# Reordering the start of an attention-plus-mixer kernel: masks first, a third decay buffer, weight conversions and products placed by hand

## The chip, the cores and the metric

One core of one Trainium2 chip. The metric is the device time of one execution in microseconds (us). Engines are named as the profile names them: PE is TensorE's matmul side, PEld its weight loads, DVE is VectorE, ACT is ScalarE, POOL is GpSimd, SP issues the DMAs. The median time of several runs is called "the median". Positions inside an execution ("103.57") are microseconds from the start of the profiled run, which is one run among several.

## The reference

An RWKV6 recurrence per head, followed by an MLP mixer over tokens and then over channels, all in float32 (the mixer's weights arrive as float64):

```python
batch, n_heads, seq, head_dim = (4, 8, 768, 48)
state = np.zeros((B, H, D, D))
for t in range(S):
    cur = np.einsum('bhd,bhe->bhde', u[None] * kt, vt)
    y[:, :, t] = np.einsum('bhd,bhde->bhe', rt, state + cur)
    state = wt[:, :, :, None] * state + np.einsum('bhd,bhe->bhde', kt, vt)
# ... y becomes x: (B, S, H*D) = (4, 768, 384)
h = np.maximum(xt @ w_tok1, 0.0) @ w_tok2          # over tokens, d_tok 256
u = x + h.transpose(0, 2, 1)
h2 = np.maximum(u @ w_ch1, 0.0) @ w_ch2            # over channels, d_ch 1536
return u + h2
```

## The kernel before

The attention is cut into 12 units, three to a batch element, of 256 tokens each. `levels(i)` makes the weights within a unit: a first block (`begin` scales r and k on ScalarE, `gram0` multiplies them, a masked copy on VectorE picks the result), then five further levels, each with a gram on PE, a *join* on VectorE (r and k multiplied by decays) and another masked copy (plain copies on ScalarE at the last two levels). `post(i)` then does the transposes, the products kv, the states, the part of y that comes from the states (`before`), a tiny copy `seen` on ScalarE (two words per partition), and the part of y from within the unit (`within`).

The first batch element (units 0 to 2) also has to convert the float64 weights. One "pair" is two pieces of 512 columns, each with one exponent step on ScalarE (L170) and five steps on VectorE (L169, 171, 172, 173, 175). There are three pairs for the token weights (`to_tok`; the texts call them pairs 1, 2 and 3, in Python `to_tok[0]` to `[2]`) and nine for the channel weights (`to_ch`).

```python
# the order of emission below, with the scheduler's own choices,
# sets the order of each engine's queue
for n, t in enumerate((rs[i % 3], ks[i % 3], ws[i % 3])):   # load_rkw
    sp.dma_start(t[rows], rkw[i, n, rows, :])
# ...
masks.append(m8)                                  # six casts on VectorE
for i, t in enumerate(weights_at):
    (dve if i == 0 else pool).memset(t, 0.0)
# ... levels(i), begin():
decay = apool.tile([128, COLS // 2], f32, name="decay")          # two buffers
rp = L["rp"] = apool.tile([128, COLS], f32, name="rp")
kp = L["kp"] = apool.tile([128, COLS], f32, name="kp", bufs=1)   # one buffer
# ... post(i), at the end of before():
seen = apool.tile([128, 2], f32, name="seen")
act.copy(seen, y[:, :, UC * A * D - 1])           # within() waits for it
# ... mixing():
def hidden(i, c):   # one w_tok1 product, 12 per batch element: 2 sums of 6
    ...
def back(c):        # two w_tok2 products, then x += on VectorE (the add, L430)
    ...
# ... the first batch element:
emit(woven(levels(0), levels(1)))
load_v(0); load_rkw(2); load_v(1); load_v(2)
p0, p1, p2 = post(0), post(1), post(2)
p1[3:3] = hiddens[0] + hiddens[1]
p2[3:3] = hiddens[2] + hiddens[3]
emit(woven(levels(2), p0 + p1, to_tok[:2]))
emit(woven(p2, to_tok[2:]))
emit(hiddens[4] + hiddens[5])
# then: six back products and turns woven with to_ch[:2], then the up products
# (z_ps), the down products, and units 3 to 11 woven into the mixing of the rest
```

Of the kernel before, what the change touches and what calls it, by code (L numbers as in the profile page):

```python
# [10 lines left out]
f32 = mybir.dt.float32  # L11
# [18 lines left out]
COLS = UC * A * 128  # L30
# [7 lines left out]
def woven(*lists):  # L38

    keyed = []  # L40
    for n, pieces in enumerate(lists):
        total, at = sum(c for c, _ in pieces), 0.0
        for i, (c, f) in enumerate(pieces):
            keyed.append(((at + c / 2) / total, n, i, c, f))
            at += c
    return [(c, f) for *_, c, f in sorted(keyed, key=lambda e: e[:3])]


def emit(pieces):
    for _, f in pieces:  # L50
        f()
# [3 lines left out]
def rwkv6_then_mixer(  # L55
# [22 lines left out]
    nc = tc.nc  # L78
    pe, dve, act, pool, sp = nc.tensor, nc.vector, nc.scalar, nc.gpsimd, nc.sync

    const = ctx.enter_context(tc.tile_pool(name="const", bufs=1))
    wts = ctx.enter_context(tc.tile_pool(name="wts", bufs=1))
    vpool = ctx.enter_context(tc.tile_pool(name="vpool", bufs=3))
    apool = ctx.enter_context(tc.tile_pool(name="apool", bufs=2))
# [8 lines left out]
    rs = [const.tile([128, COLS], f32, name=f"r{i}") for i in range(3)]  # L93
    ks = [const.tile([128, COLS], f32, name=f"k{i}") for i in range(3)]
    ws = [const.tile([128, COLS], f32, name=f"w{i}") for i in range(3)]
    weights_at = [const.tile([128, 2, UC * A, T], f32, name=f"at{i}") for i in range(3)]
    vs = {}

    def load_rkw(i):
        if i >= NU:  # L100
            return
        for n, t in enumerate((rs[i % 3], ks[i % 3], ws[i % 3])):
            for rows in (slice(0, 128),) if i < 3 else (slice(0, D), slice(P, P + D)):
                sp.dma_start(t[rows], rkw[i, n, rows, :])

    def load_v(i, queue=sp):
        if i >= NU:
            return
        vs[i] = vpool.tile([128, UC, DM], f32, name="vt")
        b, j = divmod(i, UB)  # L110
        queue.dma_start(vs[i], v[b, ts(j, UC * 128), :].rearrange("(c p) e -> p c e", p=128))

    u_col = const.tile([128, A], f32, name="u_col")
    act.dma_start(u_col, u)
    load_rkw(0)
    load_rkw(1)



    masks = []  # L120
    for l in range(4):
# [7 lines left out]
        n, x = (T, 1) if l == 0 else (32, UC * A)  # L129
# [2 lines left out]
        for j in range(2):  # L132
            dve.tensor_copy(m8[ts(j, T)], flat[ts(j, T), ts(j, n)].unsqueeze(1).to_broadcast([T, x, n]))
        masks.append(m8)
    for i, t in enumerate(weights_at):
        (dve if i == 0 else pool).memset(t, 0.0)
    ident = const.tile([128, 128], f32, name="ident")
    make_identity(nc, ident)

# [48 lines left out]
    def conversion(*weights):  # L188
        pieces = [e for w in weights for e in blocks(*w)]
        return [(0.2, lambda n=n: convert(pieces[n:n + 2], n)) for n in range(0, len(pieces), 2)]  # L190
# [6 lines left out]
    def levels(i):  # L197
# [5 lines left out]
        products = []  # L203

        def begin():
            decay = apool.tile([128, COLS // 2], f32, name="decay")
            L["w"] = apool.tile([128, UC, A, 2], f32, name="w_chunk", bufs=4)
            pool.memset(L["w"], 0.0)
            products.extend([w_, decay, w_[:, :COLS // 4], decay[:, :COLS // 8], w_[:, :COLS // 16],
                             decay[:, :COLS // 32], L["w"].rearrange("p c a j -> p (c a j)")])  # L210

            rp = L["rp"] = apool.tile([128, COLS], f32, name="rp")
            kp = L["kp"] = apool.tile([128, COLS], f32, name="kp", bufs=1)
            both = [(t.rearrange("p (n two) -> p n two", two=2)[:ROWS], x.rearrange("p (n two) -> p n two", two=2)[:ROWS], o)
                    for t, x, o in ((rp, r_, 1), (kp, k_, 0))]
            for t, x, o in both:
                act.copy(t[:, :, o], x[:, :, o])
            for t, x, o in both:
                t, x = (e[:, :, 1 - o].rearrange("p (c a n) -> p c a n", c=UC, a=A) for e in (t, x))
                for a in range(A):  # L220
                    act.mul(t[:, :, a, :], x[:, :, a, :], u_col[:ROWS, a:a + 1])  # L221
# [76 lines left out]
        def block(l):  # L298
            gram(l)
            join(l, products[l], products[l + 1])  # L300
            pick(l)

        pieces = [(0.1, begin), (1.6, first_block)]
        for l in range(1, LEVELS):
            pieces.append((1.2, lambda l=l: block(l)))
        return pieces

    def post(i):
# [69 lines left out]
        def within():  # L378
# [9 lines left out]
            for n in range(2):  # L388
                act.copy(x[ts(n, P), 1], got[ts(1 - n, P), 1])  # L389

        return [(1.0, tokens), (1.1, carry), (0.1, update), (1.1, before), (1.1, within),
                (0.01, lambda: load_rkw(i + 3)), (0.01, lambda: load_v(i + 3))]


# [9 lines left out]
    def weight_sums():  # L404
        t1, t2, t4 = w_sums
        dve.tensor_sub(t1, w12, w11)
        dve.tensor_sub(t2, w22, t1)
        dve.tensor_sub(t4, w21, t2)
# [121 lines left out]
    def beside(after, ahead):  # L530

        tokens, carry, update, before, within, *loads = after
        begin, first, *rest = ahead

        def one(*pieces):
            return (sum(c for c, _ in pieces), lambda: emit(pieces))

        return [begin, tokens, one(carry, first), update, one(before, rest[0]), one(within, rest[1]), *loads, *rest[2:]]


    hiddens, turned, ups, downs = mixing(0)
    hiddens = [list(e) for e in zip(*hiddens)]
    to_tok = conversion((wtok1, w_tok1, 2, 256), (wtok2, w_tok2, 2, 256))
    to_ch = conversion((wch1, w_ch1, 1, 512), (wch2, w_ch2, 4, 128))
    emit(woven(levels(0), levels(1)))
    load_v(0)
    load_rkw(2)
    load_v(1)
    load_v(2)
    p0, p1, p2 = post(0), post(1), post(2)  # L550
    p1[3:3] = hiddens[0] + hiddens[1]
    p2[3:3] = hiddens[2] + hiddens[3]
    emit(woven(levels(2), p0 + p1, to_tok[:2]))
    emit(woven(p2, to_tok[2:]))
    emit(hiddens[4] + hiddens[5])


    for bt in range(B):
        if bt == 0:
            emit(woven(turned, to_ch[:2]))  # L560
            both = [f for e in zip(ups[0], ups[1]) for f in e]
            emit(woven(both, to_ch[2:7]))
            emit(woven(downs[0][:-4], to_ch[7:]))
            weight_sums()
            pieces = downs[0][-4:] + [(0.01, weight_difference)] + downs[1] + ups[2] + downs[2]
        else:
            hiddens, pieces, ups, downs = mixing(bt)
            pieces = [(3.9, lambda h=h: emit(h)) for h in hiddens] + pieces
            for s in range(S // SEG):
                pieces += ups[s] + downs[s]  # L570
        n = (bt + 1) * UB
        if n < NU:
            att = levels(n) if bt == 0 else []
            for i in range(n, n + UB):
                att += beside(post(i), levels(i + 1)) if i + 1 < NU else post(i)
            emit(woven(att, pieces))
        else:
            emit(pieces)
# [29 lines left out]
```

## Time and profile before

| | before |
|---|---|
| median (4 runs) | 627.34 us (626.74 to 627.84) |
| profiled run | 625.85 us, span 624.1 us |
| first level-1 gram on PE | 15.68 |
| states of unit 2, 12 steps (L350) | 78.05 to 80.24 |
| first add to end of sixth (L430) | 91.47 to 102.87 |
| first up product (z_ps, L443) | 103.57 |
| from there to the end | 520.5 us |

The page, the stages and the chain of this run are in the prediction below. This is the timeline of the kernel before, cut to one stretch. Each line has start, length, engine, source line, operation, output and inputs, count, and in brackets the idle time of the engine just ahead and what ended it:

```profile
78.05 2.19 DVE L350 SCALAR_TENSOR_TENSOR state<-state,w_chunk,kv_ps 128x48 f32<-128x48 f32 x12 [1.51 <-PE kv_ps L333]
...
81.68 0.16 ACT L376 COPY seen<-y_ps 128x2 f32<-128x2 f32 x1 [1.22 <-PE y_ps L370]
81.90 1.96 PE L383 MATMUL y_ps<-vt,at 64*64 64x48 f32 x64
83.64 1.68 PE L256 MATMUL gram<-r,k 48*64 48x32 f32 x52
85.42 4.17 PE L421 MATMUL h_ps<-x,wtok 128*128 128x384 f32 x8
91.47 0.56 DVE L430 TENSOR_TENSOR x<-x,h_ps 128x384 f32<-128x384 f32 x1 [0.92 <-PE h_ps L428]
103.57 4.70 PE L443 MATMUL z_ps<-xT,wch 128*128 128x256 f32 x21
```

Read it from top to bottom as one path: states of unit 2, `seen`, 64 products within the unit, then a gram (of unit 3, which fills PE while ScalarE copies y into x), the last eight matmuls of w_tok1, the adds, and the first up product. The change works on every link of it.

### The profile page before, as it was taken

How to read it: one execution, taken by the hardware profiler on the slowest of the kernel's cores; microseconds unless marked ns; L12 is line 12 of the kernel's file. 1: busy time of each engine (PE TensorE's matmuls, PEld its weight loads, DVE VectorE, ACT ScalarE, POOL GpSimd, SP SyncE). 2: the span in 40 equal slices, each digit the busy share in tenths (PEclk: the TensorE clock that was granted, in tenths of full speed). 3: DMA queues.
4: the chain of work that ended last, by engine and by line, in shares of the span. 5: the costliest groups of instructions: out<-in, count | busy, mean ns of one | idle time of the engine just before them, and what ended most of it. 6: DMA issues, size and time to landing. Idle time of an engine off the chain costs nothing.

```text
span 624.1 us, 19852 instructions
## 1 busy us (share of the span) xinstructions
PE 591.5 (95%) x8980; PEld 500.7 (80%) x8980; DVE 341.5 (55%) x743; ACT 201.6 (32%) x500; POOL 7.2 (1%) x32
## 2 busy tenths in 40 slices
PE   2888788999999999999999999999999999999997
PEld 2867556876888896789889896789899885898987
DVE  5889799996766783436364362526243331040403
ACT  6064554520355433432323312332212411202020
POOL 4000000000000000000000000000000000000000
PEclk9996679999999999999999999999999999999999
DMA  8236564610232222111111100000000000000000
GB/s 344 105 80 213 162 197 141 221 43 27 65 94 79 54 67 66 30 50 27 53 45 60 27 28 27 1 2 3 26 2 27 2 27 1 0 1 26 16 12 26
DMA packets 19380, 38.63 MB, mean 62 GB/s; under 512 B 2112, under 2 KB 12864, under 8 KB 19296
## 3 DMA queue, kind: packets, MB, share of 16 engines
q1 hardware_dynamic: 19152, 37.36, 19.0%
q8 instruction: 70, 1.15, 0.8%
q14 instruction: 14, 0.11, 0.1%
q10 hardware_dynamic: 144, 0.00, 0.0%
HBM read 32.64 MB, written 4.72 MB: 60 GB/s over the span
## 4 chain that ended last, share of the span: by engine, by line
PE 88%; DVE 6%; ACT 3%; issue 1%; DMA 1%; SPq 0%; DVEq 0%; ACTq 0%
PE z_ps L443 30%; PE q_ps L477 25%; PE gram L256 8%; PE h_ps L428 5%; PE h_ps L421 5%; PE h_ps L453 3%; PE y_ps L383 2%; PE y_ps L370 2%; PE kv_ps L333 2%; PE gram L233 2%; PE kT_ps L323 1%; PE xT_ps L435 1%; PE gram L250 1%; DVE state L350 1%; DMA w<-in_rkw_dram 1%
## 5 line engine op out<-in xcount | busy, mean ns | idle before, releaser
L443 PE MATMUL z_ps<-xT,wch 128*128 128x256 f32 x864 | 195.3, 382 | 0.0
L443 PEld LDWEIGHTS z_ps<-xT,wch 128*128 128x128 f32 x864 | 161.4, 190 | 22.4 <-ACT z L445 0.7
L445 ACT ACTIVATE z<-z_ps 128x256 f32<-128x256 f32 x144 | 55.0, 382 | 159.4 <-PE z_ps L443 145.7
L477 PE MATMUL q_ps<-wch,z 128*128 128x192 f32 x528 | 93.6, 329 | 0.0
L477 PEld LDWEIGHTS q_ps<-wch,z 128*128 128x128 f32 x528 | 86.3, 190 | 1.3
L477 PE MATMUL q_ps<-scratch,z 128*128 128x192 f32 x396 | 71.1, 330 | 0.0
L256 PEld LDWEIGHTS gram<-r,k 48*64 48x64 f32 x3072 | 59.4, 153 | 13.0 <-issue 7.2
L256 PE MATMUL gram<-r,k 48*64 48x32 f32 x3072 | 64.6, 235 | 4.1 <-issue 1.8
L477 PEld LDWEIGHTS q_ps<-scratch,z 128*128 128x128 f32 x396 | 64.3, 190 | 0.9 <-ACT kT L324 0.2
L288 DVE TENSOR_TENSOR k<-k,decay 112x512 f32<-112x512 f32 x36 | 24.9, 691 | 46.1 <-PE gram L256 34.6
L469 DVE TENSOR_TENSOR z<-z 128x768 f32<-128x768 f32 x11 | 10.5, 958 | 63.5 <-ACT z L445 63.4
L288 DVE TENSOR_TENSOR k<-k,w 112x512 f32<-112x512 f32 x36 | 24.8, 690 | 35.6 <-PE gram L256 30.0
L428 PE MATMUL h_ps<-h,wtok 128*128 128x384 f32 x96 | 37.0, 510 | 3.8 <-DVE x L430 2.0
L350 DVE SCALAR_TENSOR_TENSOR state<-state,w_chunk,kv_ps 128x48 f32<-128x48 f32 x160 | 30.7, 258 | 17.3 <-PE kv_ps L333 17.3
L421 PE MATMUL h_ps<-x,wtok 128*128 128x384 f32 x96 | 37.5, 541 | 1.7 <-ACT x L389 1.6
L430 DVE TENSOR_TENSOR x<-x,h_ps 128x384 f32<-128x384 f32 x24 | 13.3, 555 | 36.6 <-PE h_ps L428 36.3
L233 PE MATMUL gram<-rp,kp 48*64 48x64 f32 x768 | 22.5, 248 | 10.9 <-ACT kp L221 8.2
L272 DVE COPY_PREDICATED at<-mask,gram 128x512 f32<-128x512 uint8 x36 | 32.3, 898 | 0.0
L233 PEld LDWEIGHTS gram<-rp,kp 48*64 48x64 f32 x768 | 18.4, 154 | 15.4 <-ACT kp L221 10.7
L421 PEld LDWEIGHTS h_ps<-x,wtok 128*128 128x128 f32 x96 | 19.2, 208 | 13.5 <-ACT x L389 2.0
L280 ACT COPY at<-gram 16x256 f32<-16x256 f32 x48 | 17.4, 363 | 36.3 <-PE gram L256 35.1
L428 PEld LDWEIGHTS h_ps<-h,wtok 128*128 128x128 f32 x96 | 16.4, 189 | 15.5 <-DVE x L430 3.3
(80 smaller groups left out, 563.0 us busy)
## 6 DMA issues: line engine op xcount, KB each, us to landing
scratch<-in_w_ch_dram SPq DMA_DIRECT2D x10, 512.0 KB, 4.4
vt<-in_v_dram SPq DMA_DIRECT2D x12, 384.0 KB, 3.7
out_dram<-o SPq DMA_DIRECT2D x24, 192.0 KB, 1.9
x<-in_w_ch_dram SPq DMA_DIRECT2D x8, 512.0 KB, 4.4
w<-in_rkw_dram SPq DMA_DIRECT2D x18, 192.0 KB, 3.3
k<-in_rkw_dram SPq DMA_DIRECT2D x18, 192.0 KB, 3.1
r<-in_rkw_dram SPq DMA_DIRECT2D x18, 192.0 KB, 3.5
scratch<-in_w_tok_dram SPq DMA_DIRECT2D x4, 512.0 KB, 9.2
```

Of the source, the lines that this page charges most:

```text
L233: pe.matmul(g[cols, q, ts(a, T)], L["kp"][rows, tokens], L["rp"][rows, tokens], start=True, stop=True)
L256: fours(lambda q, j, rows, cols: pe.matmul(g[cols, q, ts(ca, 32)], k_[rows, ds(ca * 128 + j * T, T)], right[rows, ts(2 * ca + j, 32 // b), ...
L272: dve.copy_predicated(out=dst, data=g.rearrange("p q (m b) -> p q m b", b=b), mask=masks[l].rearrange("p x t -> p (x t)").rearrange("p (m ...
L280: act.copy(at[p:p + b, :, :, n * 2 * b + b:(n + 1) * 2 * b], g[p:p + b, :, :, ts(n, b)])
L288: dve.tensor_mul(left, left, wv[:, :, 1].unsqueeze(2).to_broadcast([ROWS, n, b]))
L350: dve.scalar_tensor_tensor(new[:, a], state[bt, g][:, a], L["w"][:, c, a, j:j + 1], got[:, a], op0=ALU.mult, op1=ALU.add)
L421: pe.matmul(sums[i], wtok1[:, c, ts(i, 128)], xs[bt][:, c, :], start=(c == 0), stop=(c == C - 1))
L428: pe.matmul(ps, wtok2[:, i, ts(c, 128)], h1[:, i, :], start=(i == 0), stop=(i == DTOK // 128 - 1))
L443: pe.matmul(ps, wch1[:, m, ts(jt, 128)], xT[:, m, ts(s, SEG)], start=(m == 0), stop=(m == DM // 128 - 1))
L445: act.activation(zs[s][:, jt, :], ps, AF.Relu)
L453: pe.matmul(ps, zs[0][:, jt, ts(n, 128)], wch2[:, jt, :], start=(jt == 0), stop=(jt == NJ - 1))
L477: pe.matmul(ps, a[:, j, :], b[:, j, :], start=(j == 0), stop=(j == HJ - 1))
```

## The change

The intent: have the mask casts out of the way when the first gram is ready; let decays run ahead; keep conversions out of the way of unit 2's joins; use the room at unit 2's joins and states for token pairs 2 and 3; and put w_tok1 products into unit 2's post. Two helpers pin the order of issue: `newest` notes an engine's latest instruction, `behind` makes later pieces stand behind it in that engine's queue without any semaphore.

```diff
+    def newest(*engines):
+        return {e.engine: next(ins.name for ins in reversed(block.instructions) if ins.engine == e.engine)
+                for e in engines}
+
+    def behind(marks, pieces):
+        ...   # each instruction of the pieces is ordered after marks[its engine]
@@
+    for t in weights_at:
+        dve.memset(t, 0.0)
@@ load_rkw
-        for n, t in enumerate((rs[i % 3], ks[i % 3], ws[i % 3])):
+        for n, t in ((1, ks[i % 3]), (2, ws[i % 3]), (0, rs[i % 3])):
@@ after the masks
-    for i, t in enumerate(weights_at):
-        (dve if i == 0 else pool).memset(t, 0.0)
+    masked = newest(dve)
@@ begin
-            decay = apool.tile([128, COLS // 2], f32, name="decay")
+            decay = apool.tile([128, COLS // 2], f32, name="decay", bufs=3)
@@ the first batch element
-    emit(woven(levels(0), levels(1)))
+    emit(behind(masked, woven(levels(0), levels(1))))
     ...
-    p1[3:3] = hiddens[0] + hiddens[1]
-    p2[3:3] = hiddens[2] + hiddens[3]
-    emit(woven(levels(2), p0 + p1, to_tok[:2]))
-    emit(woven(p2, to_tok[2:]))
+    l2, joined = levels(2), {}
+    l2.append((0.01, lambda: joined.update(newest(dve))))
+    emit(woven(l2, p0 + p1, to_tok[:1]))
+    tokens, carry, update, before, within, *loads = p2
+    emit([tokens, *hiddens[0], carry])
+    emit(behind(joined, to_tok[1:2]))
+    emit([update])
+    updated = newest(dve)
+    emit(hiddens[1] + [before] + hiddens[2] + [within] + hiddens[3] + loads)
+    attended = newest(pe)
+    emit(behind(updated, to_tok[2:]))
     emit(hiddens[4] + hiddens[5])
@@ batch loop
-            att = levels(n) if bt == 0 else []
+            att = behind({**updated, **attended}, levels(n)) if bt == 0 else []
```

In what follows, **the opening** is the first part (memsets, casts first, load order, `behind(masked, …)`), **the decay** is the third buffer, and **the placing** is everything from `l2, joined` on, the last line included.

## The prediction

> **What bounds the kernel now.** I read the page's first two parts for the engines and the stages, then the chain that ended last in order of time, then windows by stage and the timeline of the first 105 us. The page:
>
> ```profile
> PE 591.5 (95%) x8980; PEld 500.7 (80%) x8980; DVE 341.5 (55%) x743; ACT 201.6 (32%) x500; POOL 7.2 (1%) x32
> PE   2888788999999999999999999999999999999997
> DVE  5889799996766783436364362526243331040403
> PEclk9996679999999999999999999999999999999999
> ```
>
> One slice is 15.6 us. TensorE is full from slice 7 on (104 us), and everything the change could win lies in the first seven slices, where VectorE is at 8 to 9 and TensorE has gaps. The windows say it in us (columns: busy time and instructions of PE, PEld, DVE, ACT, POOL, then clock, DMA share, GB/s):
>
> ```profile
> 8.00:44.00 36.00, 28.52 (x932) 26.00 (x936) 31.85 (x65) 16.61 (x44) 0.00 (x0) 1.00 0.48 167
> 44.00:90.00 46.00, 38.09 (x958) 28.93 (x950) 41.87 (x110) 23.02 (x54) 0.34 (x3) 0.70 0.60 183
> 90.00:104.00 14.00, 11.33 (x44) 6.49 (x43) 12.28 (x25) 6.69 (x16) 0.00 (x0) 1.00 0.42 130
> 104.00:150.00 46.00, 46.00 (x233) 35.66 (x233) 41.48 (x72) 16.26 (x37) 0.00 (x0) 1.00 0.34 109
> ```
>
> PE's idle time before 104 us is 8.2 + 7.5 + 7.9 + 2.7 = 26 us; after it, 520 us hold some 6.4 us of idle. VectorE is idle for 10 us between 8 and 104. So the end is set by when the first `up` product (z_ps, L443) starts, now 103.6 us, plus a TensorE-bound rest which the change does not touch in kind. The chain shows the alternation ahead of it (start, length, what):
>
> ```profile
> 10.20 0.70 DVE decay L290
> 11.88 1.33 DVE at L239 x2
> 15.68 2.78 PE gram L256 x94
> 68.53 1.65 PE h_ps L421 x2
> 78.05 2.20 DVE state L350 x12
> 85.39 0.53 ACT scratch L170
> 97.67 0.57 DVE x L430
> 103.73 31.48 PE z_ps L443 x144
> ```
>
> The readings are that the opening waits on VectorE (the mask casts, run from 8.59 to 11.9 beside the decay products, hold the first masked copies back), that unit 2's states come late (78.05), since two conversions of token weights stand in VectorE's queue between unit 2's joins, and that channel-weight conversions (L170, L173) then mix with the back products.
>
> [...] the decay product ran at 10.20 although its input was read by the join at 7.38, because six casts stood ahead. So the order of issue, which this change pins, is worth as much as the dependencies. [...] the clock in the windows 48-50 and 50-54 is 0.50. [...] the clock column reads 1.00 from 0 to 44 us, yet a gram of 64 matmuls takes 1.97 us there (23.49) against 1.14 us at 149 us, so I take the opening for half clock as well. [...]
>
> **Part 1: masks first, three memsets on VectorE, k before w before r.** VectorE has 5.4 us of wait before 7.38; in it now go 3 memsets of 0.91 (two were GpSimd's) and the casts, 1.59 + 0.58. They need the masks, and GpSimd, freed of its memsets, should end at about 5.4. VectorE is then free at about 6.2. That takes 2.2 us off the path from the first join to the first masked copy. But a load of 512 KB takes 1.28 us (first ready at 4.74, 5.99, 7.38), so r of unit 0 comes at 7.25 in place of 4.7, and ScalarE's queue now reads: kp copy and 4 scalings (0.65 + 1.33), rp copy at 7.3, 4 scalings to 9.3, then **kp of unit 1, which has a single buffer** and waits for the last of unit 0's 64 products. Those end at 9.3 + 0.3 + 1.1 = 10.7. Then kp copy 0.65, rp copy 0.65, rp scalings 1.3: unit 1's first product at 13.6, its last at 14.6 + 0.3 + 1.1 = 16.0, against 15.1 now. The gram of level 1 starts there: 16.0 against 15.68. **Sum: +0.3 us**; the casts' gain is eaten by the load order and the single kp.
>
> **Part 2: three decay buffers.** Unit 2's first decay product and first join (0.65 each) move from 33 to 39 us into the opening, at about 16. VectorE then is ahead by 1.3 us at 38 us, less the r join that stays. It removes no wait of the chain: **about 0 to -0.5 us**.
>
> **Part 3: the placing of token pairs and products.** The compiled order, engine by engine, shows VectorE doing pair 1 as now, then unit 2's levels 1 to 5 without a conversion between levels 3 and 5, then pair 2 around the last join, the states of unit 2, pair 3, and only then unit 3's first block. I walk VectorE's new queue with the durations of the old trace (join half 0.61, masked copy 0.65, level 1's 1.28, 12 state steps 2.17, 16 steps 2.88, a conversion step pair 0.7, 0.7, 1.2, 1.2, 1.2). From 38.3: level 1's join at 48.5 (now 49.3). There y of unit 0 and its within products are put before most of the level-2 gram on TensorE, at half clock 1.95 us each, so level 2's join comes at 54.4 (now 53.7), and level 3's, after two products of w_tok1 (0.73 each warm, 1.5 cold), at 59.9 (now 58.3). VectorE idles some 2.5 and 3.4 us there, since pair 2's work no longer fills the gap. Level 5's join then comes at 68 to 69, now 71.04: without pair 2 ahead of it **2.5 us are won**. Of that ScalarE takes back: its queue has the exponent step of pair 2 ahead of the one-word copy `seen` that frees the within products of unit 1, and w_tok1 products of unit 1 stand ahead of unit 2's kv. The states of unit 2 come at 76 to 77.3 (now 78.05), the last w_tok1 product ends at 87.6 to 89 (now 89.6). One exponent step (0.7) no longer stands between the two ReLUs of h1. First L430: 88.7 to 90.5 against 91.47. **Sum: -1 to -2.8 us.**
>
> **Part 4: what was displaced.** In the old order 7 us of channel-weight conversion lie before the first L430. In the new one none does, so it falls among the six L430 (0.5 each): between the second and third stand 4.3 us of conversion steps, between the fourth and the sixth 5.5. TensorE needs 2.45 us from one back product to the next, so it waits. From the first L430 to the end of the sixth: two pairs at 5.0 + 6 x 0.5 + one wait of 0.9 = 13.9 us, now 91.47 to 102.87 = 11.4. **Sum: +2.5 us.** After that VectorE is one pair (5 us) behind, ending its conversions at 138 in place of 132.6. That is hidden: the last channel weights are first read 8 x 1.18 = 9.4 us into the down products, which start at 135.2.
>
> **The sum.** +0.3 - 0.3 - 1.9 + 2.5 = +0.6 us: a first `up` product at 104.2, 627.8 us. It is a long walk with some ten waits, good to 3 us.
>
> **Rivals.** (1) *The clock.* Half clock shows in 47-57, 66-76 and 83-88 us, some 20 us of PE work which would take about 11 at full clock. [...] one spell of 10 us spared gives 3 to 5 us, of which perhaps half on the chain. [...] Against: new waits of VectorE for TensorE mean that neither overlaps better. Time then: 623 to 625. (2) *VectorE stays the bound and all is moved, not removed.* Its work before 132 us is the same, plus 1.8 us of memsets in idle time. For it: DVE at 8 to 9 tenths until slice 9. Then 627 to 628. (3) *Back products stall more than I say*, because scratch and spare are loaded late: the first channel pair's buffers come free only after pair 3 (about 85), and a load of two took some 4.5 us. Then the first up product comes at 106 to 107, and the time is 630. (4) *The opening wins its 2 us after all*, if ScalarE's kp of unit 1 isn't held. Then 625 or 626.
>
> **Range and chances.** The walk gives 627.8. Rival 1 seems to me the likelier of the departures (one in two, -4), rivals 3 and 4 one in five each (+2.5, -2). That makes 627.8 - 2.0 + 0.5 - 0.4 = 625.9. The range is 5 to either side: 620.5 to 631. A gain of over 2% is 12.5 us, half of all the idle time ahead of 104 us, for a change that removes no work: 0.03. A loss of as much would need stalls far beyond rival 3: 0.02.
>
> **What would show it right or wrong.** In the changed kernel: VectorE free of casts by 6.3 us, the first masked copy at 9.6 to 10, but the first level-1 gram between 15.5 and 16.3. The states of unit 2 (12 steps) at 76 to 77.5. First L430 (a few lines lower in the new source) at 88.7 to 90.5. The third L430 over 4 us after the second, with PE waiting for VectorE there. First z_ps product between 101 and 106.5, and from there to the end 520 us as now. It is wrong if the first z_ps product comes before 99 us (the clock or pair 2's place won more), if the opening ends over 1.5 us earlier, or if the rest after it isn't 520 us, which would mean that the later order of decays and joins counts.

## The result and the profile after

| | before | after |
|---|---|---|
| median (4 runs each) | 627.34 us | 630.21 us (629.19 to 630.57) |
| profiled run | 625.85 us | 630.19 us |

The ratio of the times is 1.0044, with a 95% interval of 1.0026 to 1.0061: within 2%, but slower. A ratio here is the mean time of one kernel's fast runs over that of the other's fast runs of the same rounds, so it is not quite the ratio of the medians quoted. The profiled run of the kernel before is faster than all four runs of its median, so the two profiles differ by 4.3 us where the medians differ by 2.9.

Three of the lines of the page that the prediction shows, for the changed kernel:

```profile
PE 591.7 (94%) x8980; PEld 500.6 (80%) x8980; DVE 343.3 (55%) x745; ACT 201.1 (32%) x500; POOL 6.6 (1%) x30
DVE  7886769999676783635454471616344341040403
PEclk9996769999999999999999999999999999999999
```

PE's busy time is the same (591.5 and 591.7), so nothing was added or taken away: the time lost is waiting. VectorE is emptier in the fourth and the sixth slice (47 to 63 and 79 to 94 us: 6 tenths in place of 9) and fuller in the tenth (141 to 157 us: 9 in place of 6). The windows put it in numbers, with the columns of the prediction's windows:

```profile
8.00:44.00 36.00, 28.13 (x912) 25.78 (x916) 31.05 (x58) 16.65 (x44) 0.00 (x0) 1.00 0.47 167
44.00:90.00 46.00, 34.66 (x905) 26.70 (x898) 34.60 (x92) 20.42 (x49) 1.50 (x3) 0.73 0.56 165
90.00:104.00 14.00, 12.77 (x101) 7.21 (x100) 9.71 (x21) 6.68 (x14) 0.00 (x0) 0.93 0.27 92
104.00:150.00 46.00, 44.23 (x188) 34.73 (x188) 46.00 (x85) 18.45 (x40) 0.00 (x0) 1.00 0.43 138
```

Between 44 and 90 us VectorE did 34.60 us of work in place of 41.87, and PE 34.66 in place of 38.09. Of the displaced VectorE work 4.5 us lies in the last window; another 4.2 us had moved into the first 8 us, where the fills and casts now run. Source lines in the new kernel are 19 higher (the add is L449, z_ps L462). The timeline of the changed kernel over the same path as before:

```profile
76.89 2.19 DVE L369 SCALAR_TENSOR_TENSOR state<-state,w_chunk,kv_ps 128x48 f32<-128x48 f32 x12 [1.21 <-PE kv_ps L352]
...
79.51 1.34 ACT L189 ACTIVATE scratch<-scratch,rebias 128x512 uint16<-128x512 uint16 x2
81.05 0.14 ACT L395 COPY seen<-y_ps 128x2 f32<-128x2 f32 x1
81.24 0.43 PE L402 MATMUL y_ps<-vt,at 64*64 64x48 f32 x12 [0.86 <-ACT seen L395]
83.51 1.73 PE L402 MATMUL y_ps<-vt,at 64*64 64x48 f32 x52 [1.84 <-issue]
86.78 5.46 PE L440 MATMUL h_ps<-x,wtok 128*128 128x384 f32 x8 [1.54 <-ACT x L408]
94.23 0.55 DVE L449 TENSOR_TENSOR x<-x,h_ps 128x384 f32<-128x384 f32 x1 [5.03 <-PE h_ps L447]
...
107.67 0.60 PE L462 MATMUL z_ps<-xT,wch 128*128 128x256 f32 x2
```

Follow the path against the one before:

| link | before | after | change of lead |
|---|---|---|---|
| states start | 78.05 | 76.89 | −1.2 |
| `seen` after y's end (81.64, 80.37) | +0.04 | +0.68 | +0.6 |
| within products | 1.96 in one run | 0.43, stall 1.84, 1.73 | +2.0 |
| w_tok1's last eight matmuls | 4.17 | 5.46 | +1.3 |
| first add to end of sixth | 11.40 | 12.94 | +1.5 |
| first z_ps | 103.57 | 107.67 | **+4.1** |
| z_ps to the end | 520.5 | 520.8 | +0.3 |

The rows up to the adds sum to +2.7; the first add came 2.76 later. The states won what was hoped for. Then it was given back four times over: `seen` stood behind two exponent steps on ScalarE (L189, both of pair 3's) and one scaling of unit 3's kp, PE stopped for 1.84 us *in the middle of* 64 independent products with nothing to wait for ("issue"), the w_tok1 products ran at half clock longer, and the adds were stretched by channel conversions. VectorE did no work from 89.2 to the add at 94.23: the conversion that followed stood behind the add in VectorE's own queue and ran at 94.70.

The clock records explain the fourth row. The last stretch at half clock is 81.30 to 88.13 (6.83 us) in the kernel before and 81.84 to 92.08 (10.24 us) in the changed one. The stretch before it is the other way round: 64.23 to 74.47 (10.24 us) and 68.18 to 75.01 (6.83 us). The recorded half clock of the two runs is the same in sum, 27.31 us; it lies at another place of the path. So these two runs show that the last link is slower, not that the clock took time from the whole. Windows of the two, kernel before first:

```profile
86.00:90.00 4.00, 4.00 (x10) 1.88 (x8) 4.00 (x10) 1.69 (x5) 0.00 (x0) 0.73 0.67 197
90.00:94.00 4.00, 3.35 (x12) 1.75 (x11) 2.95 (x6) 2.76 (x8) 0.00 (x0) 1.00 0.38 127
```

```profile
86.00:90.00 4.00, 3.22 (x5) 1.83 (x6) 3.20 (x6) 1.39 (x3) 0.00 (x0) 0.50 0.83 299
90.00:94.00 4.00, 4.00 (x28) 1.96 (x27) 0.00 (x0) 2.18 (x6) 0.00 (x0) 0.74 0.17 64
```

The third column from the end is the clock: 0.73 and 1.00 in the first, 0.50 and 0.74 in the second.

What is the 1.84 us stall? I listed every idle gap of PE above 0.4 us ahead of 108 us that the trace marks "issue", with the number of the instruction in PE's own queue (matmuls, weight loads and PE's semaphore instructions all counted, from 0). In the two kernels these are, with length in us:

```
before  449 (1.02)  2753 (0.75)
after   449 (1.43)  3009 (0.75)  3521 (1.84)
```

All these numbers leave 193 when divided by 256, and so did every such stall in all later runs, with one exception: in eight of them a gap of 0.45 to 0.67 us ahead of a transpose, at 35 to 38 us, is marked "issue" too, but stands at another remainder and moves with its product. The page's third part has this queue:

```profile
q8 instruction: 70, 1.15, 0.8%
```

70 packets, 1.15 MB: 16,384 bytes each, and 70 x 256 is 17,920, against 17,960 matmuls and weight loads (18,049 records with the semaphore instructions). So by count one packet comes to 256 PE instructions; that is an estimate of mine from these numbers, and no view shows what a packet holds. The trace does show when the packets came. In the changed kernel a packet began at 81.08 and took 1.11 us, PE stopped at 81.67 and resumed at 83.51, 1.3 us after the packet's end. In the kernel before, the packet ahead of the same index took 1.42 us from 78.76; PE reached the index only at 81.72, 1.5 us after the packet's end, and ran on. The same order holds in all 14 traces: with packets and places counted in order, there are 968 crossings of such a place, PE passed none sooner than 1.20 us after the end of its packet (1.39 in the kernel before, 1.26 in the changed one), and each of the 40 stalls over 0.4 us ahead of 108 us ended 1.20 to 1.80 us after one. So the stall seems to end 1.2 to 1.8 us after the packet, whenever PE arrives; then the table's +0.6 for `seen` and +2.0 for the stall are one loss, set by the packet: an earlier `seen` would only have let PE stand longer. That a late packet is the cause is an inference of mine from this order in time, and no view shows it; the experiments below move the stall. Why the changed kernel's packet began 2.3 us later than the one before is not shown.

### The profile page after: what moved, and what is told of

It is laid out like the page before. It is cut to its first block, busy times and chain, and to the rows that moved or that the text cites. A ratio compares the mean times of both kernels' runs of the same rounds, so it can differ in the third digit from the quotient of the medians.

```text
span 628.5 us, 19858 instructions
## 1 busy us (share of the span) xinstructions
PE 591.7 (94%) x8980; PEld 500.6 (80%) x8980; DVE 343.3 (55%) x745; ACT 201.1 (32%) x500; POOL 6.6 (1%) x30
## 3 DMA queue, kind: packets, MB, share of 16 engines
q8 instruction: 70, 1.15, 0.8%
## 4 chain that ended last, share of the span: by engine, by line
PE 85%; DVE 8%; ACT 3%; issue 3%; DMA 1%; SPq 0%; DVEq 0%; ACTq 0%
PE z_ps L462 28%; PE q_ps L496 25%; PE gram L275 8%; PE h_ps L440 6%; PE h_ps L447 4%; PE y_ps L402 3%; PE h_ps L472 2%; PE gram L252 2%; PE y_ps L389 2%; PE kv_ps L352 2%; PE kT_ps L342 1%; DVE state L369 1%; DVE wch L194 1%; PE gram L269 1%; DMA r<-in_rkw_dram 1%
## 5 line engine op out<-in xcount | busy, mean ns | idle before, releaser
L462 PE MATMUL z_ps<-xT,wch 128*128 128x256 f32 x864 | 195.3, 382 | 0.1
L462 PEld LDWEIGHTS z_ps<-xT,wch 128*128 128x128 f32 x864 | 161.4, 190 | 22.6 <-ACT z L464 0.8
L449 DVE TENSOR_TENSOR x<-x,h_ps 128x384 f32<-128x384 f32 x24 | 13.2, 553 | 40.0 <-PE h_ps L447 39.9
L308 DVE TENSOR_TENSOR r<-r,w 112x512 f32<-112x512 f32 x36 | 24.7, 686 | 7.6 <-ACT rp L236 7.6
```

The lines of the kernel that those rows point to most:

```text
L308: dve.tensor_mul(right, right, wv[:, :, 0].unsqueeze(2).to_broadcast([ROWS, n, b]))
L462: pe.matmul(ps, wch1[:, m, ts(jt, 128)], xT[:, m, ts(s, SEG)], start=(m == 0), stop=(m == DM // 128 - 1))
```

## The experiments

Twelve kernels were run, all with right results. Each was timed against the kernel before on the same chip; "before" below is that median. The theory at the start was that the placing makes the loss, through the stall, the late `seen` and the adds, and that the opening wins nothing because of its load order. The rivals were: the opening or the decay loses; the loss is VectorE's conversions alone, moved behind the first add; the loss is the clock alone.

| run | median us | before us | ratio, 95% | states end | first add to sixth's end | first z_ps | span |
|---|---|---|---|---|---|---|---|
| opening_alone | 627.38 | 626.75 | 1.0016 [0.9997, 1.0034] | 82.27 | 94.89–106.3 | 106.98 | 627.7 |
| placing_alone | 629.46 | 626.75 | 1.0036 [1.0020, 1.0052] | 79.46 | 94.36–107.6 | 108.15 | 628.8 |
| fill | 629.28 | 626.75 | 1.0043 [1.0027, 1.0059] | 80.18 | 92.84–103.7 | 104.19 | 626.9 |
| after_rkw | 626.93 | 626.75 | 1.0006 [0.9992, 1.0019] | 76.86 | 91.77–105.0 | 105.54 | 626.2 |
| opening_rkw | 625.68 | 625.95 | 0.9991 [0.9963, 1.0018] | 78.80 | 91.33–102.7 | 103.43 | 624.3 |
| seen_first | 629.09 | 625.95 | 1.0044 [1.0015, 1.0073] | 79.33 | 92.73–105.8 | 106.35 | 627.0 |
| shift40 | 629.14 | 625.95 | 1.0038 [0.9997, 1.0080] | 75.61 | 88.01–101.2 | 101.79 | 622.6 |
| all_four | 626.92 | 625.95 | 1.0006 [0.9978, 1.0033] | 75.92 | 90.96–102.0 | 102.56 | 625.6 |
| unit3_ahead | 628.90 | 626.33 | 1.0049 [1.0029, 1.0070] | 78.28 | 92.85–106.2 | 106.76 | 626.6 |
| unit3_ahead_rkw | 627.89 | 626.33 | 1.0027 [1.0007, 1.0046] | 77.37 | 90.43–104.6 | 105.15 | 624.8 |
| decay_alone | 626.62 | 626.33 | 1.0012 [0.9992, 1.0032] | 79.91 | 91.25–102.6 | 103.34 | 624.0 |
| rkw_shift20 | 630.00 | 626.90 | 1.0044 [1.0004, 1.0083] | 76.08 | 89.11–102.4 | 102.89 | 624.3 |

A caution for the table: the last four columns are from one profiled run each, and that run may lie at either end of its kernel's runs (those of opening_alone, placing_alone and after_rkw are the slowest, those of shift40, decay_alone and unit3_ahead_rkw the fastest). The ratio decides; the profile says where.

### opening_alone and placing_alone

One half of the change each, on the kernel before. The first:

```diff
+    for t in weights_at:
+        dve.memset(t, 0.0)
-        for n, t in enumerate((rs[i % 3], ks[i % 3], ws[i % 3])):
+        for n, t in ((1, ks[i % 3]), (2, ws[i % 3]), (0, rs[i % 3])):
-    for i, t in enumerate(weights_at):
-        (dve if i == 0 else pool).memset(t, 0.0)
+    masked = newest(dve)
-    emit(woven(levels(0), levels(1)))
+    emit(behind(masked, woven(levels(0), levels(1))))
```

> The kernel before with the opening alone: three zero fills on VectorE, mask casts first, loads in the order k, w, r. Theory A (casts' gain is eaten by the load order and the single kp buffer): first level-1 gram at 15.5 to 16.0 us (before 15.68, changed kernel 15.70), states of unit 2 as before (done 80.2), total within 1 us of the kernel before. Rival (the opening costs the change its loss through later order): 629 to 630 us, first up product 2 us later than 103.6.

The second is the two last parts of the diff above (from `l2, joined` to `to_tok[2:]`, and the `behind` in the batch loop), with the opening and the decay as before.

> The kernel before with the placing of the token pairs and products alone (opening and decay buffers as before). Theory A (the placing is the loss): 629.5 to 630.5 us; first L430-type add after 93.5 us, third of them over 3 us after the second, first up product near 107.5. Rival (it is the sum of parts, or the opening): 627 to 628 us.

The opening alone gave 1.0016, with an interval that includes no change, and a first level-1 gram at 15.44. The placing alone gave 1.0036, 2.7 us by the medians, with stalls of 1.67 and 1.98 us at the same two places as in the changed kernel (67 and 82 us). So of the parts tried alone the placing is the only one whose interval lies wholly above 1. A small loss by the opening, up to some 2 us, isn't excluded: its profiled run, the slowest of its six, had unit 2's states end at 82.27 (expected: 80.2) and the first z_ps at 106.98, behind a half-clock stretch of 17.07 us (48.15 to 65.21). There the profile looks like the rival, and the six times do not.

### decay_alone

```diff
-            decay = apool.tile([128, COLS // 2], f32, name="decay")
+            decay = apool.tile([128, COLS // 2], f32, name="decay", bufs=3)
```

> The kernel before with three decay buffers in place of two and nothing else. Theory A (no wait of the chain was on a decay buffer): within 0.7 us of the kernel before, first up product at 103 to 104. Rival (the later units gain from it): 1 us or more faster, won after 150 us.

Ratio 1.0012, interval over 1 to both sides, first z_ps at 103.34 against 103.57. The third buffer does nothing that can be measured.

### after_rkw and opening_rkw

The load order r, k, w of the kernel before, put back into the changed kernel (after_rkw), and the opening alone with it (opening_rkw):

```diff
-        for n, t in ((1, ks[i % 3]), (2, ws[i % 3]), (0, rs[i % 3])):
+        for n, t in enumerate((rs[i % 3], ks[i % 3], ws[i % 3])):
```

> The changed kernel with unit loads in the old order r, k, w. Theory A (r last and the single kp hold unit 1's first products back): unit 1's first products start at 11.4 to 12 us, first level-1 gram at 13.3 to 14 us (now 15.70), and what follows moves with it: about 2 us less, 628 us. Rival (ScalarE is not the holder): first level-1 gram at 15.3 or later, time as the changed kernel.

> The kernel before with masks cast first and the zero fills on VectorE, but loads in the old order r, k, w, and nothing else. Theory A (casts first is worth 2 us as long as the load order stays): first level-1 gram at 13.7 to 14.1 us, 2 to 2.5 us under the kernel before, 624 to 625 us, the best so far. Rival (the lead is lost in the queues before unit 2's states): 626 to 627 us.

The opening of PE's timeline in the kernel before (which waits for the masked copy, L239):

```profile
12.76 2.33 PE L233 MATMUL gram<-rp,kp 48*64 48x64 f32 x64 [2.29 <-DVE at L239]
15.68 2.57 PE L256 MATMUL gram<-r,k 48*64 48x32 f32 x88 [0.59 <-DVE at L239]
```

In the changed kernel (which waits for ScalarE's kp of unit 1; that copy starts 0.12 us after unit 0's 64 products, the first line, end):

```profile
8.31 2.24 PE L252 MATMUL gram<-rp,kp 48*64 48x64 f32 x64 [8.31 <-ACT rp L240]
10.67 0.65 ACT L236 COPY kp<-k 112x512 f32<-112x512 f32 x1 [1.51 <-issue]
13.45 2.26 PE L252 MATMUL gram<-rp,kp 48*64 48x64 f32 x64 [2.90 <-ACT kp L240]
15.70 2.57 PE L275 MATMUL gram<-r,k 48*64 48x32 f32 x88
```

And in after_rkw:

```profile
11.62 2.25 PE L252 MATMUL gram<-rp,kp 48*64 48x64 f32 x64 [1.28 <-ACT kp L240]
13.90 2.78 PE L275 MATMUL gram<-r,k 48*64 48x32 f32 x94
```

One wait had taken the place of another: the casts ended at 6.57 in place of 11.9, the first masked copy came at 9.76 in place of 11.88, and PE then waited 2.90 us for kp. With the old load order 1.8 us of it are won at the first level-1 gram, and the changed kernel is 2.4 us nearer to the kernel before (1.0006 in place of 1.0044, in different rounds). So this one line takes back most of the loss although the whole placing stays in. What the placing costs on this opening is the difference between 0.9991 (opening_rkw, below) and 1.0006; the intervals tell it neither from zero nor from the 1.0036 that it cost on the old opening.

On the kernel before, the same opening starts the first level-1 gram at 13.74 and gave 0.9991, i.e. nothing that can be told from zero. Its lead is lost at the end of the path:

```profile
80.57 1.96 PE L402 MATMUL y_ps<-vt,at 64*64 64x48 f32 x64
84.23 5.49 PE L440 MATMUL h_ps<-x,wtok 128*128 128x384 f32 x8 [0.24 <-ACT x L408]
103.43 4.92 PE L462 MATMUL z_ps<-xT,wch 128*128 128x256 f32 x22
```

It was 1.3 us ahead at the within products, but the eight w_tok1 matmuls took 5.49 us in place of 4.17: its last half-clock stretch is 79.93 to 90.17, so 10.24 us in place of 6.83. The first z_ps is back at 103.43.

These two kernels are also the cleanest pair for the placing (with the decay buffer): same opening, and the last half-clock stretch 10.24 us in both (the one before it is not the same: 10.24 us in opening_rkw, 6.83 in after_rkw). Here is after_rkw:

```profile
79.02 0.43 PE L402 MATMUL y_ps<-vt,at 64*64 64x48 f32 x12 [0.86 <-ACT seen L395]
81.35 1.73 PE L402 MATMUL y_ps<-vt,at 64*64 64x48 f32 x52 [1.90 <-issue]
105.54 2.76 PE L462 MATMUL z_ps<-xT,wch 128*128 128x256 f32 x12
```

With the last half-clock stretch equal, the placing is −1.9 at the states (76.86 against 78.80), +0.6 at `seen`, +1.9 for the stall, −0.3 in the w_tok1 products, +1.9 in the adds (13.27 against 11.36): +2.1 at the first z_ps and +1.9 in the span. (By the medians of their rounds, which were not the same ones, it is 1.3 us, and after_rkw's profiled run was its slowest.)

### fill

This gives VectorE the first channel pair before the adds, in the stretch where it had been idle, by using the other half of the buffers for it:

```diff
-        return [(0.2, lambda n=n: convert(pieces[n:n + 2], n)) ...]
+        return [(0.2, lambda n=n: convert(pieces[n:n + 2], n + at)) ...]
-    to_ch = conversion((wch1, w_ch1, 1, 512), (wch2, w_ch2, 4, 128))
+    to_ch = conversion((wch1, w_ch1, 1, 512), (wch2, w_ch2, 4, 128), at=2)
+    emit(to_ch[:1])                     # after emit(behind(updated, to_tok[2:]))
-            emit(woven(turned, to_ch[:2]))
+            emit(woven(turned, to_ch[1:2]))
```

> The changed kernel, with the first pair of channel weights converted before the back products, out of the buffer that is free first. Theory A (displaced conversions cost 1.5 us between the first and the sixth add: 12.9 us now, 11.4 before): that stretch falls to 11 to 11.6, first add stays at 94.2, first up product near 106.2, total 628.5 to 629. Rival 1 (conversions do not matter, the late within products of unit 2 are all of the loss): unchanged at 630.2. Rival 2 (the pair now delays the first add): 630 or more.

The adds shrank as they should (10.9 us in place of 12.94), and the first z_ps came at 104.19 in place of 107.67. But the time stayed at 1.0043. From the first z_ps to the end it took 522.7 us, not 520.8: 768 gram matmuls had run ahead of that point where the changed kernel has 832, and those 64 (1.14 us at full clock) now came later, beside larger gaps (3.69 us in sum, against 3.30). So 1.9 of the 3.5 us gained at z_ps were lost again after it, most of that as work pushed past the point at which I measured. Of the 3.5 us, 1.4 were there at the first add already (92.84, expected: 94.2), since the stall was only 0.56 us in this run. The rest of the gain shows in the profiled span (626.9 against 628.5), not in the ratio.

### seen_first

`seen` is put ahead of the exponent steps in ScalarE's queue:

```diff
-    emit(hiddens[1] + [before] + hiddens[2] + [within] + hiddens[3] + loads)
+    emit(hiddens[1] + [before])
+    seen = newest(act)
+    emit(hiddens[2] + [within] + hiddens[3] + loads)
-    emit(behind(updated, to_tok[2:]))
+    emit(behind({**updated, **seen}, to_tok[2:]))
```

> The changed kernel with pair 3's two exponent steps on ScalarE behind the two-column copy that frees unit 2's within products. Theory A (the copy stood 0.7 us behind them): the copy runs within 0.1 us of the end of y (80.4), the within products start 0.5 to 0.7 us earlier; total 629.5. Rival: the stall of PE after 12 within products grows by as much as is won, 630.2.

The copy came 0.22 us after y's end in place of 0.68 (behind four scalings of unit 3's kp), the stall was still there (1.45 us), and the ratio is again 1.0044. The wait of `seen` is real, and removing it is worth nothing that can be measured while the stall follows it.

### shift40 and rkw_shift20

If the stall belongs to a place in PE's queue, instructions added at the front must move it to other products. Both kernels add 20 small products of zeros at the very start (40 matmuls, 2.34 us, and 40 weight loads in the trace), shift40 to the changed kernel, rkw_shift20 to after_rkw:

```diff
+    zero = const.tile([32, 32], f32, name="zero")
+    dve.memset(zero, 0.0)
+    idle = ps_g.tile([128, 2, 512], f32, name="gram")
+    for n in range(20):        # 80 instructions in PE's queue
+        pe.matmul(idle[:32, 0, :32], zero, zero, start=True, stop=True)
```

> The changed kernel with 20 small products of zeros (40 matmuls, 40 weight loads) added at PE's start, which no result reads; PE's instruction stream is 80 longer ahead of everything. Theory A [...]: the stall leaves that place, for one some 40 matmuls earlier or none, and the last w_tok1 product of unit 2 ends 1 to 2 us earlier than 92.2; total 628.5 to 629.5. Rival (the stall is a wait for data of the within products): it stays after 12 to 13 products, time 630 or more.

> The changed kernel with the old load order, and 20 small products of zeros at PE's start that no result reads (80 instructions). Here the compiled order of every engine is otherwise that of the kernel with the load order alone[...]. Theory A [...]: no stall inside the within products of units 1 and 2, first up product 1 to 2.5 us before 105.54, total 624.5 to 626 us against 626.9. Rival [...]: stall gone, total 627.

In both the stall left the within products of unit 2. In rkw_shift20, whose compiled order is otherwise that of after_rkw:

```profile
79.10 1.75 PE L407 MATMUL y_ps<-vt,at 64*64 64x48 f32 x64 [0.26 <-ACT seen L400]
82.40 4.74 PE L445 MATMUL h_ps<-x,wtok 128*128 128x384 f32 x8 [1.55 <-ACT x L413]
102.89 5.35 PE L467 MATMUL z_ps<-xT,wch 128*128 128x256 f32 x24
```

64 products in one run, and the first z_ps 2.65 us earlier than in after_rkw. The stalls are now at indices 705 (1.32), 1985 (1.88), 2753 (1.99) and 3521 (1.16), which again all leave 193 (besides the gap at the transpose, 0.67); index 3521 falls into other products:

```profile
78.17 0.67 PE L394 MATMUL y_ps<-state,r 48*64 48x48 f32 x28 [1.16 <-issue]
```

So its place is settled: the stall belongs to a place in PE's queue, not to a product or a tile.

What it is worth in time is not settled. The two medians got no better (629.14 and 630.00), with a wide spread: rkw_shift20's six runs lie between 623.34 and 632.51. The mean clocks of its fastest and slowest run (0.992, 0.975) decide nothing, since the clock records of different runs do not begin at the same place (last section). The stalls at these places sum to 6.35 us in it and to 4.12 in after_rkw: others came for the one removed.

### all_four

After_rkw with both edits of seen_first and fill.

```diff
-        for n, t in ((1, ks[i % 3]), (2, ws[i % 3]), (0, rs[i % 3])):
+        for n, t in enumerate((rs[i % 3], ks[i % 3], ws[i % 3])):
+    seen = newest(act)                  # with the rest of seen_first
-    to_ch = conversion((wch1, w_ch1, 1, 512), (wch2, w_ch2, 4, 128))
+    to_ch = conversion((wch1, w_ch1, 1, 512), (wch2, w_ch2, 4, 128), at=2)
+    emit(to_ch[:1])                     # with the rest of fill
```

> The changed kernel with the old load order, the copy ahead of pair 3's exponents, and the first channel pair converted before the back products. If the three gains add (3.0, 0.6, 1.0 us): 625.5 us, level with or under the kernel before. If late work is only put off into the TensorE-bound rest: 627, as with the load order alone.

1.0006, as after_rkw alone. Its first z_ps came at 102.56, 3 us earlier than after_rkw's, and its stall was the longest (2.92 us); the rest took 523.0 us (again 768 gram matmuls ahead of z_ps). That the gains add up does not show.

### unit3_ahead and unit3_ahead_rkw

In the kernel before, a gram of unit 3 filled PE's wait ahead of w_tok1 (83.64 to 85.4). The placing orders unit 3 behind, so that wait (1.54 us in the changed kernel) was empty. The suspicion was that this gap lengthens the half-clock stretch. The edit puts the head of unit 3 ahead of pair 3:

```diff
+    l3 = behind({**updated, **attended}, levels(3))
+    emit(l3[:2])
     emit(behind(updated, to_tok[2:]))
-            att = behind({**updated, **attended}, levels(n)) if bt == 0 else []
+            att = l3[2:] if bt == 0 else []
```

> The changed kernel with unit 3's first block (join, decay, two masked copies) ahead of pair 3 in VectorE's queue, so that its level-1 gram can again stand on PE between unit 2's within products and the last w_tok1 products, as in the kernel before, and unit 3's level-1 join fills VectorE's 5 us wait. Theory A (part of the loss is PE standing idle there[...]): last half-clock spell 6.83 us in place of 10.24, last w_tok1 product ends at 90 to 91 (now 92.2), total 628 to 628.7. Rival (the clock does not hang on that wait): spell of 10.24 us, time 630 as now, or later by pair 3's delay.

> The same with unit loads in the old order r, k, w as well. If the two gains add: 2.4 us under the one above, 625.5 to 626.3 us, under or level with the kernel before. Rival [...]: 627 us, as with the load order alone.

The gram did fill the wait (unit3_ahead):

```profile
84.16 1.98 PE L275 MATMUL gram<-r,k 48*64 48x32 f32 x60
86.07 5.24 PE L440 MATMUL h_ps<-x,wtok 128*128 128x384 f32 x8
```

But the matmuls after it still took 5.24 us, and the half-clock stretch was 10.24 us all the same (80.70 to 90.94). The time stayed at 1.0049. In unit3_ahead_rkw the stretch was 6.83 us (80.50 to 87.33), and its ratio is 1.0027 nevertheless. So filling that one gap isn't what brings the clock back, and what does is open.

## Why the prediction was right and wrong

The range (620.5 to 631) and "within 2%" held: 630.21 lies in it, near the upper end. The expected 625.9 was 4.3 us too low, and the walk itself (627.8) 2.4 us too low. By its steps:

- **Part 1, the opening, +0.3: held, with its mechanism.** The first level-1 gram came at 15.70 (said: 16.0, before 15.68), the first masked copy at 9.76 (said: 9.6 to 10), unit 1's first product at 13.45 (said: 13.6). Of the named cause, r last is confirmed by after_rkw and opening_rkw: 13.90 and 13.74 with the old load order. The single kp is seen in the trace alone (the copy at 10.67, right after unit 0's products); no run gave kp a second buffer. The casts ended at 6.57, said 6.3.
- **Part 2, the decay, 0 to −0.5: held** (decay_alone).
- **Part 3, the placing, −1.9: this is the step that failed.** Its first half was right, link by link: the joins of levels 2 and 3 at 53.93 and 59.34 (said: 54.4 and 59.9), VectorE's waits there 2.70 and 3.38 (said: 2.5 and 3.4), the states at 76.89 (said: 76 to 77.3). Its second half, that w_tok1 would end at 87.6 to 89 and the first add come at 88.7 to 90.5, was not: 92.24 and 94.23. Measured in the profiled runs it is +2.8 at the first add. The walk carried the lead of the states through `seen`, the within products and w_tok1 with old durations. It left out three things: ScalarE's exponent steps ahead of unit 2's `seen` (it has this wait for unit 1 only), 0.6 us; the stop in PE's queue at index 3521, 2.0 us; the longer last half-clock stretch, 1.3 us (a shorter stretch ahead of the states may have helped their lead). The prediction's rule "the order of issue is worth as much as the dependencies" applied to the very copy it overlooked.
- **Part 4, the displaced conversions, +2.5: right in kind, mis-sized.** The third add came 4.76 us after the second (said: over 4). The stretch from the first to the sixth add took 12.94 us in place of 11.40, so 1.5 more and not 2.5. The mis-sized term is the wait: the sum was two pairs at 5.0, six adds at 0.5 and one wait of 0.9, and VectorE did not wait once, as the lines below show: no line after the first has a wait in brackets. Without the 0.9 the sum is 13.0. It also said that VectorE would then be 5 us behind and end its conversions at 138; they ended at 141.86, 9.2 us later than before (132.63). That this would be hidden held: 520.8 us from the first z_ps to the end.

```profile
94.23 0.55 DVE L449 TENSOR_TENSOR x<-x,h_ps 128x384 f32<-128x384 f32 x1 [5.03 <-PE h_ps L447]
94.70 0.42 DVE L188 TENSOR_SCALAR scratch<-scratch 128x512 uint16<-128x512 uint16 x1
...
95.52 0.55 DVE L449 TENSOR_TENSOR x<-x,h_ps 128x384 f32<-128x384 f32 x1
...
100.28 1.01 DVE L449 TENSOR_TENSOR x<-x,h_ps 128x384 f32<-128x384 f32 x2
...
103.16 0.54 DVE L449 TENSOR_TENSOR x<-x,h_ps 128x384 f32<-128x384 f32 x1
...
106.63 0.54 DVE L449 TENSOR_TENSOR x<-x,h_ps 128x384 f32<-128x384 f32 x1
```

- **The sum, +0.6:** +4.1 at the first z_ps in the profiled runs, 2.9 by the medians. The first z_ps at 107.67 is outside the 101 to 106.5 that was said, the 520 us after it held (520.8).
- **The rivals.** The clock (1) was given one chance in two, as a *gain*. That the new order would bring one was an estimate, and no run shows what sets the clock. No such gain came: the recorded half clock is 27.31 us in both runs, with the longer stretch now at the end (10.24 in place of 6.83), where it slowed w_tok1. (The prediction put the half clock of the kernel before at 47 to 57, 66 to 76 and 83 to 88 us; the records have it at 47.17 to 57.41, 64.23 to 74.47 and 81.30 to 88.13. Ahead of 43.75 us, where the prediction reads the clock column's 1.00, there is no record, see the last section.) Rival 2 (moved, not removed) describes Part 4. Rival 3 had the right time (630), but not the right cause: the first channel conversion ran right behind the add, at 94.70, with its data there; it waited for no load. Rival 4 (the opening wins 2 us) did not come, and after_rkw shows the one line that held it back at the first level-1 gram.

What stays open is above all the step from the path to the time. The profiles show where the lead was given back; but the edits aimed at these links (seen_first, fill, shift40, unit3_ahead) brought no time back that can be measured (1.0044, 1.0043, 1.0038, 1.0049), and the load order, which is none of them, brought 2.4 us. Open too: the time that the stall itself costs (its place could be moved, but the moved kernels spread over 8 to 9 us); what ends a half-clock stretch after 6.83 or 10.24 us; and why after_rkw and rkw_shift20, which differ by 20 products of zeros, part by 3 us in their medians (1.0006 and 1.0044). No version clearly beats the kernel before: the best, opening_rkw, is at 0.9991, and its interval includes 1.

## What to carry to other kernels

When you walk a path into its changed order, take every queue that the path crosses, tiny copies on ScalarE included, and give each link a new duration: the lead of 1.2 us at the states was no lead at the next links here, where PE stopped for 1.84 us and the last stretch at half clock was 10.24 us in place of 6.83. Where a bound is a chain through several engines, measure a part of the change on its own first; here one line (the load order) was worth 2.4 us, and the part that looked best in the walk was the part that lost when tried alone. And choose the point at which you compare with care: an earlier "first product" may mean only that other work was put behind it.

## What the stalls and the clock records of these runs show

- PE stopped for 0.4 to 2.9 us at instructions of its queue whose number leaves 193 on division by 256, two to five times ahead of 108 us in all but one run, all of them in stretches of small matmuls (1.84 us in the changed kernel, around a packet of 1.11 us; no stop at the same index in the kernel before, where the packet had ended 1.5 us earlier). In the whole run the kernel before has two such stops over 0.4 us and the changed one three, at 70 packets each.
- Every half-clock stretch that ends inside the recorded run of the kernel before and of the changed one is 6.83 or 10.24 us long, and full work does not end them at once. In the kernel before PE was busy 4.00 of 4.00 us in the window below, and also in the one after it (54 to 58), yet the clock was 0.50 until 57.41:

```profile
50.00:54.00 4.00, 4.00 (x148) 4.00 (x152) 3.77 (x7) 1.74 (x4) 0.00 (x0) 0.50 0.53 133
```

- The clock record of these runs lacks the opening, and what is lacking counts as full clock. The first record begins at 43.75 us in the kernel before (44.29 in the changed one), and ahead of it the column reads 1.00, although a gram of 64 matmuls takes 1.97 us there and 1.14 us at full clock (149.33, clock 1.00). In decay_alone it begins only at 57.21. Its later half-clock stretches are those of the kernel before, 10.24 and 6.83 us; the place of the first, of 10.24 us, lies ahead of the record, and the mean clock reads 0.986 in place of 0.978. So mean clocks of these runs can't be compared.
